# A retention and two-layer MLP kernel on one core: each load of q, k, n, v and raw weights waits for an older load

## Chip, core and metric

The kernel runs on one core of one Trainium2 chip. The metric is the device time of one execution in microseconds (us), as a median over executions. TensorE (PE) multiplies matrices, VectorE (DVE), ScalarE (ACT) and GpSimd (POOL) work on tiles in SBUF, and SyncE (SP) computes nothing here: it issues transfers (DMAs), one after the other, in program order. An instruction on SP that waits for a semaphore holds up every transfer that is queued behind it on SP.

## The reference, cut to what matters

```
for t in range(S):                       # B, H, S, D = 2, 8, 768, 64
    state = gamma * state + einsum('bhd,bhe->bhde', k[:, :, t], v[:, :, t])
    y[:, :, t] = scale * einsum('bhd,bhde->bhe', q[:, :, t], state)
x = y.transpose(0, 2, 1, 3).reshape(1536, 512)
x = ((x @ w_a) * (x @ w_b)) @ w_out                  # 512 -> 1536 -> 512
h = x @ w_in                                          # 512 -> 2048
out = maximum(0.01 * h, h) @ moe2_w_out               # 2048 -> 512
```

All inputs and the output are float32.

## The kernel before

The work has three stages. The first one, retention, is done in 12 units: three tiles of 512 tokens by four pairs of heads. Each unit needs four tiles of 128x512 float32 (256 KB each): q and k (transposed), n (k in its plain layout) and v. The second stage is the product with w_a and w_b, the product of the two results and the product with w_out; the third is the last two products. Products are written as three matmuls over a high and a low part of each operand, and from the second stage on many are regrouped so that seven block products do the work of eight.

The weights arrive as raw 64-bit-typed tiles of 128x512 elements (512 KB each), named raw_a, raw_b, raw_wo, raw_wi and raw_wq. ACT and DVE turn each raw tile into a float32 tile; there are NRAW = 4 raw buffers, and `load_weights` issues the next raw load when one comes free.

`manual_schedule` is on, so each engine runs its instructions in the order in which the Python program emits them. All the loads of this case are issued on SP. `loads(u)` (line 519) issues the four loads of unit u, in the order q, k, n, v for units 0 to 3 and n, v, q, k for the others. The program starts with the loads of units 0 to 4, then the raw loads a0, b0 and a1 among the loads of units 5 and 6, and in the main loop (line 1067) unit u calls `loads(u + 8)`, the first pass also `load_weights()`. In all, 48 loads of 256 KB and six of 512 KB (a0, b0, a1, b1, a2, b2) are issued before 46 us. The framework gives the transfers of SP and ACT eight semaphores in turn, and a transfer waits for the one that had the same semaphore before it. Two transfers of ACT (table and rest, small constants) share these semaphores at the start.

The first matmuls of the second stage (line 1016, pa and pb) run inside the retention stage, as soon as the weights a0 and b0 are split and unit 3 is done. Here ACT's lines 316, 318 and 320 and DVE's lines 334, 336 and 338 turn a raw tile into float32; ACT's line 989 and DVE's line 996 split it; ACT's lines 539 and 603 scale n; POOL's and DVE's lines 545 and 608 scale q.

After the loads of unit 11 and the raw tiles a2 and b2, SP's queue holds only raw loads, tiles that were parked in DRAM and are fetched back (farh, farg, wi, wq; lines 454 and 777), and the stores of the output.

Of the kernel before, what the change touches and what calls it, by code (L numbers as in the profile page):

```python
# [35 lines left out]
NRAW = 4  # L36
NEXTRA = 10
NWARM = 10
FILL = {4: 4, 5: 6, 6: 6, 7: 6, 8: 6, 9: 6, 10: 6, 11: 4}
PUMP = {7: 1.2, 8: 1.6, 9: 1.2, 10: 1.2, 11: 1.2}  # L40
ROUND = {3: ("a", 0, 3), 4: ("b", 0, 3), 5: ("a", 1, 3), 6: ("b", 1, 3)}
# [50 lines left out]
class Seven:  # L92
# [41 lines left out]
    def sum(self, queue, op, j, d, x0, x1, here=False):  # L134

        run = self.nc.vector.tensor_add if op == "+" else self.nc.vector.tensor_sub
        if d[0] == "B":
            queue.append((0.34, lambda: run(*(self.B(*x[1:], j) for x in (d, x0, x1)))))
            return
        for piece, cost in enumerate((0.61, 0.34)):  # L140
            if self.away(*d[1:], j) and not piece:
                continue
            if here:
                queue.append((cost, lambda piece=piece: run(*(self.A(*x[1:], j)[piece] for x in (d, x0, x1)))))
                continue
            queue.append((0.0, lambda piece=piece: self.nc.gpsimd.dma_start(  # L146
                self.A(*d[1:], j)[piece], self.A(*x1[1:], j)[piece], accum_op=ALU.add
            )))
# [81 lines left out]
def retention_moe_kernel(ctx: ExitStack, tc: tile.TileContext, ins, out):  # L230
    nc = tc.nc
# [44 lines left out]
    first_layer = len(order)  # L276
    order += second
    source = {"a": (wab, 0), "b": (wab, 1), "wo": (wo, 0), "wi": (w2, 0), "wq": (w2, 1)}
    raws, begun, rounded, dram = {}, {}, {}, {}
    at = {"load": 0, "begin": 0, "round": 0, "queued": 0, "hold": True}  # L280

    def wait_for(later, done):
        tc.add_manual_dep(
            later.ins, done.ins.name,
            mybir.DependencyInfo(mybir.DependencyClass.Sync, mybir.DependencyReason.DATA),
        )

    def load_weights(behind=()):
        if at["load"] < len(order) and at["load"] < at["round"] + NRAW:
            kind, f = order[at["load"]]  # L290
            src, i = source[kind]
            t = rawp.tile([P, TT], I64, tag="raw", name=f"raw_{kind}{f}")
            load = nc.sync.dma_start(t, src[f, i])
            if behind:
                wait_for(load, behind[-1])
            raws[kind, f] = t
            at["load"] += 1
# [26 lines left out]
    def round_steps():  # L324


        n = at["round"]
        key = order[n]
        if key not in begun:
            begin_weights()  # L330
        u, sl = begun.pop(key)
        raws.pop(key)
        ui = u.bitcast(I32)
        nc.vector.tensor_scalar(u, u, TOP, None, op0=ALU.min)
        yield
        nc.vector.tensor_scalar(ui, ui, 3, None, op0=ALU.logical_shift_left)
        yield
        nc.vector.tensor_tensor(ui, ui, sl, op=ALU.add)
        rounded[key] = u
        at["round"] += 1  # L340
        if not at["hold"]:
            load_weights()
        if key in parked:
            dram[key] = park.tile([P, TT], F32, tag=f"{key[0]}{key[1]}", name=f"{key[0]}{key[1]}")
            nc.gpsimd.dma_start(dram[key], rounded.pop(key))
            slots.done(1)
# [160 lines left out]
    units = [(n, p) for n in range(NTILE) for p in range(NPAIR)]  # L507
# [11 lines left out]
    def loads(u):  # L519
        if u >= len(units):  # L520
            return
        d = un[u] = {}
        source = {"q": qT, "k": kT, "n": kn, "v": vn}
        for name in "qknv" if u < NPAIR else "nvqk":
            d[name] = slots.new(F32, f"{name}{u}")
            nc.sync.dma_start(d[name], source[name][units[u]])

    flip = heads[::-1]
    cols = [slice(j * P, (j + 1) * P) for j in range(CPT)]
# [434 lines left out]
    nc.vector.memset(warm, 0.0)  # L964
    nc.scalar.dma_start(table, head)
    loads(0)
    nc.scalar.copy(carry[0][0][:, 0:1], warm[:, 1:2])
    nc.scalar.dma_start(rest, more)
# [3 lines left out]
    def keep_warm(n):  # L972
        for _ in range(n):
            nc.tensor.matmul(wps, warm[:, 0:P], warm, start=True, stop=True)

    keep_warm(NWARM)
    for u in range(1, 4):
        loads(u)
    loads(4)
    load_weights()  # L980
    loads(5)
    load_weights()
    loads(6)
    load_weights()
# [78 lines left out]
    def fill(u):  # L1063
        for _ in range(FILL.get(u, 0)):
            next(dense)
# [258 lines left out]
    for n in range(NMADE, len(z.plan) - 2):  # L1324
# [12 lines left out]
        name, j = z.plan[n]  # L1337
# [195 lines left out]
    for n in range(NMADE2, len(z.plan) - 2):  # L1533
# [14 lines left out]
        name, j = z.plan[n]  # L1548
# [80 lines left out]
```

## Time and profile before

| | |
|---|---|
| median of 3 runs | 557.0 us (556.24 to 559.15) |
| profiled execution, its own time | 557.07 us |
| span of the profile | 555.3 us |
| granted TensorE clock | 1.0 |
| PE busy | 548.9 us (99%) |
| DVE, ACT, POOL busy | 457.5, 385.8, 158.9 us |
| moved by all DMAs | 108.19 MB, of them 66.60 MB from SP's queue |

The span runs from the first instruction to the last one of the profiled execution; 1.8 us of that execution's time lie outside it. Times in the rows are counted from the start of the span.

### The profile page before, as it was taken

The numbers are of one execution on the slowest core, as the hardware profiler recorded it, in microseconds if no ns is written. First come the engines' busy times: TensorE is split into PE (matmuls) and PEld (weight loads), VectorE is DVE, ScalarE is ACT, GpSimd is POOL, SyncE is SP. The second block draws the span as 40 slices with busy tenths as digits, with TensorE's granted clock in tenths as the row PEclk, the third lists the DMA queues.
The fourth block names the chain that finished last, engine by engine and source line by source line (L and its number), as shares of the span: only waits on it lengthen the run. The fifth ranks groups of instructions, "written<-read, shape, count | busy, mean of one in ns | idle before, by whom it ended". The sixth has DMA issues, their size and how long they took to land.

```text
span 555.3 us, 10484 instructions
## 1 busy us (share of the span) xinstructions
PE 548.9 (99%) x3743; PEld 462.5 (83%) x3743; DVE 457.5 (82%) x973; ACT 385.8 (69%) x797; POOL 158.9 (29%) x203
## 2 busy tenths in 40 slices
PE   8999999999999999999999999999999999999997
PEld 5878888888888888888888888888888888888886
DVE  4877967889898898899789859896977798999862
ACT  4867377877789888867758457769766886687800
POOL 3524201113231430267520320221433556700000
PEclk9999999999999999999999999999999999999999
DMA  8996934548788987899992362665787799964111
GB/s 313 393 375 167 217 93 119 154 133 212 195 253 219 259 220 253 260 305 240 243 186 94 66 125 71 184 181 158 231 240 233 206 272 242 223 164 118 58 58 57
DMA packets 49765, 108.19 MB, mean 195 GB/s; under 512 B 5936, under 2 KB 13360, under 8 KB 49712
## 3 DMA queue, kind: packets, MB, share of 16 engines
q1 hardware_dynamic: 27360, 66.60, 36.7%
q0 software_dynamic: 22064, 40.64, 34.5%
q8 instruction: 29, 0.48, 0.3%
q10 hardware_dynamic: 288, 0.28, 0.2%
q14 instruction: 24, 0.20, 0.1%
HBM read 73.68 MB, written 18.35 MB: 166 GB/s over the span
## 4 chain that ended last, share of the span: by engine, by line
PE 95%; DMA 3%; DVE 1%; issue 0%; ACT 0%; SPq 0%
PE blk L258 12%; PE blk L257 12%; PE blk L259 12%; PE top L257 6%; PE top L258 5%; PE top L259 5%; PE pa L257 4%; PE pa L259 4%; PE pa L258 4%; PE pb L257 4%; PE pb L259 4%; PE pb L258 4%; PE mid L257 3%; PE mid L259 3%; PE mid L258 3%; DMA q<-in_qT 2%
## 5 line engine op out<-in xcount | busy, mean ns | idle before, releaser
L258 PE MATMUL blk<-form,form 128*128 128x512 f32 (+1 forms) x224 | 75.8, 339 | 0.0
L257 PE MATMUL blk<-form,form 128*128 128x512 f32 (+1 forms) x224 | 75.6, 337 | 0.0
L259 PE MATMUL blk<-form,form 128*128 128x512 f32 (+1 forms) x224 | 75.3, 336 | 0.0
L173 DVE TENSOR_TENSOR form<-g,form 128x512 fp32r<-128x512 f32 x112 | 57.6, 551 | 0.9
L258 PE MATMUL blk<-forma,forma 128*128 128x512 f32 (+1 forms) x168 | 56.9, 338 | 0.0
L257 PE MATMUL blk<-forma,forma 128*128 128x512 f32 (+1 forms) x168 | 56.7, 337 | 0.0
L259 PE MATMUL blk<-forma,forma 128*128 128x512 f32 (+1 forms) x168 | 56.4, 336 | 0.0
L167 ACT CAST form<-g 128x512 fp32r<-128x512 f32 x112 | 52.4, 512 | 4.7 <-DMA g<-g 2.8
L257 PEld LDWEIGHTS blk<-form,form 128*128 128x128 f32 x224 | 42.5, 190 | 5.3
L173 DVE TENSOR_TENSOR forma<-h,forma 128x512 fp32r<-128x512 f32 x84 | 43.0, 551 | 4.5 <-ACT forma L167 3.0
L258 PEld LDWEIGHTS blk<-form,form 128*128 128x128 f32 x224 | 42.5, 190 | 4.7
L259 PEld LDWEIGHTS blk<-form,form 128*128 128x128 f32 x224 | 42.3, 189 | 4.8
L167 ACT CAST forma<-h 128x512 fp32r<-128x512 f32 x84 | 38.8, 511 | 2.8 <-DMA h<-h 2.8
L763 POOL DMA_DIRECT2D farg<-g x26 | 15.6, 616 | 80.7 <-ACT g L1373 62.8
L146 POOL DMA_DIRECT2D h<-h x33 | 33.0, 1133 | 14.3 <-DVE forma L173 3.9
L257 PEld LDWEIGHTS blk<-forma,forma 128*128 128x128 f32 x168 | 31.9, 190 | 3.9
L258 PEld LDWEIGHTS blk<-forma,forma 128*128 128x128 f32 x168 | 31.9, 190 | 3.6
L259 PEld LDWEIGHTS blk<-forma,forma 128*128 128x128 f32 x168 | 31.7, 189 | 3.6
L763 POOL DMA_DIRECT2D farh<-h x19 | 11.0, 576 | 74.6 <-DVE h L893 50.3
L173 DVE TENSOR_TENSOR form<-wq,form 128x256 fp32r<-128x256 f32 x56 | 23.4, 418 | 10.0 <-ACT form L167 9.9
L167 ACT CAST form<-wq 128x256 fp32r<-128x256 f32 x56 | 22.6, 403 | 6.3 <-PE blk L258 2.8
L146 POOL DMA_DIRECT2D g<-farg x22 | 22.0, 1040 | 9.1 <-DVE form L173 5.6
(3062 smaller groups left out, 1680.4 us busy)
## 6 DMA issues: line engine op xcount, KB each, us to landing
raw_wi<-in_w SPq DMA_DIRECT2D x16, 512.0 KB, 4.3
raw_wq<-in_w SPq DMA_DIRECT2D x16, 512.0 KB, 5.0
farg<-g POOLq DMA_DIRECT2D x26, 256.0 KB, 4.5
g<-farg SPq DMA_DIRECT2D x26, 256.0 KB, 6.6
raw_a<-in_wab SPq DMA_DIRECT2D x12, 512.0 KB, 4.5
raw_b<-in_wab SPq DMA_DIRECT2D x12, 512.0 KB, 4.9
raw_wo<-in_wo SPq DMA_DIRECT2D x12, 512.0 KB, 5.0
g<-farg POOLq DMA_DIRECT2D x20, 256.0 KB, 8.8
```

The source lines that it names most:

```text
L146: queue.append((0.0, lambda piece=piece: self.nc.gpsimd.dma_start(self.A(*d[1:], j)[piece], self.A(*x1[1:], j)[piece], accum_op=ALU.add)))
L167: nc.scalar.copy(h, src)
L173: nc.vector.tensor_sub(*todo.pop(0))
L257: nc.tensor.matmul(ps, w[0], x[0], start=first, stop=False, skip_group_check=more)
L258: nc.tensor.matmul(ps, w[0], x[1], start=False, stop=False, skip_group_check=more)
L259: nc.tensor.matmul(ps, w[1], x[0], start=False, stop=last, skip_group_check=more)
L763: nc.gpsimd.dma_start(self.far[t, f], self.tiles[t, f])
```

## The change

Each load of q, k, n, v and each raw load is entered in a list with its size in units of 256 KB (1, or 2 for a raw tile). When the loads behind the oldest one of the list, the new load among them, come to FLYING = 5 units or more, the new load waits until the oldest has landed, and the list is shortened until the rest is under 5 units. In a row of 256 KB loads, each so waits for the fifth before it. A raw load among them waits for the fifth before it too; since it counts as two, the next three loads wait for the fourth before them, and the one after these has no such wait of its own. In a row of raw loads alone, each waits for the third before it. Other transfers are neither counted nor made to wait by the list.

```diff
+FLYING = 5
...
-    raws, begun, rounded, dram = {}, {}, {}, {}
+    raws, begun, rounded, dram, aloft = {}, {}, {}, {}, []
...
+    def fly(load, size):
+        aloft.append((load, size))
+        if sum(n for _, n in aloft[1:]) >= FLYING:
+            wait_for(load, aloft.pop(0)[0])
+            while sum(n for _, n in aloft[1:]) >= FLYING:
+                aloft.pop(0)
...
             load = nc.sync.dma_start(t, src[f, i])
+            fly(load, 2)
             if behind:
                 wait_for(load, behind[-1])
...
-            nc.sync.dma_start(d[name], source[name][units[u]])
+            fly(nc.sync.dma_start(d[name], source[name][units[u]]), 1)
```

## Rows read from the trace of the kernel before

**Rows 1.** The page, part 1: busy us, share, instructions.

```profile
PE 548.9 (99%) x3743; PEld 462.5 (83%) x3743; DVE 457.5 (82%) x973; ACT 385.8 (69%) x797; POOL 158.9 (29%) x203
```

**Rows 2.** By stretches: us; PE, PEld, DVE, ACT, POOL busy; PEclk, DMA share, GB/s.

```profile
10.00:15.00 5.00, 4.58 (x88) 3.96 (x86) 2.94 (x7) 3.45 (x9) 2.55 (x2) 1.00 1.06 398
...
5.00:45.00 40.00, 37.97 (x836) 31.52 (x835) 31.08 (x73) 28.16 (x56) 15.45 (x15) 1.00 1.02 377
...
46.00:555.30 509.30, 506.09 (x2896) 428.79 (x2894) 424.49 (x897) 356.17 (x739) 141.03 (x180) 1.00 0.70 181
```

**Rows 3.** The chain that ended last, its start: start us, us, what.

```profile
2.59 5.28 DMA q<-in_qT
7.88 5.51 DMA q<-in_qT
13.41 6.65 DMA raw_a<-in_wab
20.09 0.69 ACT a L316
```

**Rows 4.** SP's timeline, issues of loads: start us, us, what.

```profile
12.05 0.33 SPq L526 DMA_DIRECT2D q<-in_qT  x1
12.73 0.33 SPq L526 DMA_DIRECT2D k<-in_kT  x1
13.41 0.33 SPq L293 DMA_DIRECT2D raw_a<-in_wab  x1
...
25.61 0.33 SPq L293 DMA_DIRECT2D raw_b<-in_wab  x1
...
37.09 0.33 SPq L526 DMA_DIRECT2D v<-in_vn  x1
...
40.28 0.38 SPq L293 DMA_DIRECT2D raw_b<-in_wab  x1
...
208.85 0.33 SPq L293 DMA_DIRECT2D raw_wo<-in_wo  x1
...
215.86 0.33 SPq L293 DMA_DIRECT2D raw_wq<-in_w  x1
```

**Rows 5.** DMA issues of 0-1, 1.6-2, 8-13 us: KB, median us to landing.

```profile
q<-in_qT SPq DMA_DIRECT2D x1, 256.0 KB, 3.2
...
n<-in_kn SPq DMA_DIRECT2D x1, 256.0 KB, 4.2
...
q<-in_qT SPq DMA_DIRECT2D x2, 256.0 KB, 5.8
```

**Rows 6.** The same of 497 to 500 us and of 119 to 119.5 us.

```profile
g<-farg SPq DMA_DIRECT2D x4, 256.0 KB, 2.7
...
raw_a<-in_wab SPq DMA_DIRECT2D x1, 512.0 KB, 3.1
```

**Rows 7.** The same at 25.6, 34 to 38.5, 40.3 and 208.9 us.

```profile
raw_b<-in_wab SPq DMA_DIRECT2D x1, 512.0 KB, 6.6
...
v<-in_vn SPq DMA_DIRECT2D x1, 256.0 KB, 5.1
...
raw_b<-in_wab SPq DMA_DIRECT2D x1, 512.0 KB, 6.0
...
raw_wo<-in_wo SPq DMA_DIRECT2D x1, 512.0 KB, 5.9
```

**Rows 8.** ACT's timeline, first use of raw a0, b1 and b2.

```profile
20.09 0.68 ACT L316 ACTIVATE a<-raw_a 128x512 f32<-128x512 f32 x1 [0.43 <-DMA raw_a<-in_wab]
...
33.84 0.70 ACT L316 ACTIVATE b<-raw_b 128x512 f32<-128x512 f32 x1
...
48.92 0.68 ACT L316 ACTIVATE b<-raw_b 128x512 f32<-128x512 f32 x1
```

## The prediction

> **What bounds the kernel now.** I read the page's busy times first: PE is busy for 548.9 of 555.3 us [rows 1]. Then I asked for busy time by stretches, to find where the missing 6.4 us are. From 46 us on PE idles for 509.30 - 506.09 = 3.2 us, which are spread over 500 us [rows 2]; between 5 and 45 us it idles for 40.00 - 37.97 = 2.03 us; the rest lies ahead of the first data. So two different kernels stand one behind the other: 46 us of retention, in which the DMA engines are as full as PE (a share of 1.06 and 398 GB/s between 10 and 15 us, 377 GB/s as a mean from 5 to 45 us), and 509 us in which PE alone sets the pace, with 181 GB/s beside it [rows 2]. The granted clock is 1.00 in all these stretches.
>
> The third view is the chain that ended last. Up to 20 us it is nothing but loads: a q issued at 2.59 that takes 5.28 us, a q issued at 7.88 that takes 5.51, and raw_a issued at 13.41 that takes 6.65; then ACT turns raw_a into float32 [rows 3]. This chain has to be read with care. Each of its links is the eighth transfer behind the one before: the issue at 7.88 comes 0.01 us after the landing of the load of 2.59, because it takes over that load's semaphore. So the queue is limited already, to eight loads or 2 MB, and SP is not ahead of the engines by more. The 5 to 7 us from issue to landing are then mostly time in the queue: loads are issued 0.68 us apart in the steady stretch (12.05, 12.73, 13.41 [rows 4]), eight of them make 5.4 us, and the view of DMA issues gives 5.8 us to landing there [rows 5]. What sets the time of a landing is how many bytes go before it, and not how early it was asked for.
>
> **The change part by part.** It removes no transfer, changes no size and no order; it adds waits on SP. There are two places to look at: the 54 loads before 46 us, and the raw loads after.
>
> After 46 us a raw load waits for the third before it. The tightest place that I found is the raw_wq issued at 215.86: the third before it is the raw_wo issued at 208.85 [rows 4] that takes 5.9 us [rows 7], so it lands at 214.75, 1.1 us before its successor would be issued anyway. All the others have more, since a raw load waits for a raw buffer and so for ACT's work. Sum of this part: 0. The cover is that buffer wait; were it gone, at most these raw loads would go out some us later, 10 us and more ahead of their use in a queue that runs behind PE.
>
> Before 46 us the waits do bite: eight loads in flight become five. (Around a raw tile, which counts as two, it is up to six units, 1.5 MB; the bound is not sharp.) The waiting instruction holds up all that is queued behind it on SP, and until 46 us these are only the next loads. Now the question is whether the engines run dry. Five loads 0.68 us apart cover 5 x 0.68 = 3.4 us. A load starves the engines only if it needs more than that from its issue to its landing when nothing is ahead of it in the queue. No row shows five in flight at full rate, so I bound it. From below: 2.7 us, for loads of the same 256 KB from a nearly empty queue [rows 6]. From above: 4.2 us, for the third load of the program [rows 5]; it has two loads and the two tables ahead of it, so a good part of that is queue. Between the two lies the very first load, with 3.2 us [rows 5], with ACT's two table loads beside it. I take the value that the row of the empty queue gives, since that row measures just the part that isn't queue, with SP, the engines and the landing in it: 2.7 us, 0.7 under the 3.4. The queue then never runs dry, loads land 0.68 us apart as before, and each at its old time. Only the time to landing falls, from 5.8 to about 3.4 us. The first five loads are issued as before, so the start is the same too.
>
> I check the late side for the last loads. The raw tile b2 now waits for v of unit 11, which is issued at 37.09 [rows 4] and takes 5.1 us [rows 7]: it goes out at 42.2 in place of 40.28. With the 3.1 us of a raw tile in an empty queue [rows 6] it can land at 45.3; before, it landed at 40.28 + 6.0 = 46.3 [rows 4, 7], and ACT takes it up at 48.92 [rows 8]. Hidden, with over 2 us to spare.
>
> What does a landing cost if it does come late? The raw tile a0 has no cover: ACT waits 0.43 us for it [rows 8], and its chain leads on to PE. The 17 units of 256 KB from the q that lands at 7.87 (2.59 + 5.28) to raw a0, landing at 20.06 (13.41 + 6.65 [rows 3]), make 12.2 us, so each 0.01 us more per load costs 0.17 us. Later tiles have some cover: raw b1 lands at 25.61 + 6.6 = 32.2 [rows 4, 7] and is taken up at 33.84 [rows 8], 1.6 us later.
>
> Sum: 0 + 0 + 0, on a profiled execution of 557.07 us (555.3 of span and 1.8 around it), which is the median of the runs, 557.0.
>
> **A rule that speaks against it.** The rows say that 2.7 us of a load are not queue [rows 6], but they say it at a low load. The Trainium skill, DMA: Bandwidth & Descriptors, section "Latency and other measured facts", gives the HBM access latency as 0.2 us on average and 2 us at high load. An estimate by that page would put the time of a lone load at 2.7 + 1.8 = 4.5 us at full rate, over the 3.4, so 0.90 us per load; raw a0 would be 17 x 0.22 = 3.7 us late and raw b1 35 x 0.22 - 1.6 = 6.1 us, and the kernel would take some 563 us. No row here shows five loads in flight at full rate, so the trace can't refute it; this is the first rival.
>
> **The rivals.**
> *The engines starve* (slower). The mechanism: time to landing at full rate is over 3.4 us even with a short queue; from there on, each load costs a fifth of it. Against it speaks the 2.7 us; for it, that the first load took 3.2 us, and that nothing shows a loaded engine. At the upper bound of 4.2 us it is 0.84 per load, 0.16 more. Raw a0 then is 17 x 0.16 = 2.7 us late: 559.7. If the delay lasts up to raw b1, 35 units after that q, it is 35 x 0.16 - 1.6 of cover = 4.0 us: 561.0. With 3.5 us, just over the edge, it is 0.02 x 17 = 0.3 us, which nobody sees. Chance 0.11.
> *The shorter queue makes landings more even* (faster). From 7.87 to 20.06 the 17 units took 12.2 us, where 17 x 0.68 are 11.6: some 0.6 us went to irregular landings. If fewer loads in flight cure that, raw a0 lands earlier, but ACT gains only its wait of 0.43 us: 556.6. The ceiling is all the idle time of PE between 5 and 45 us, 2.03 us: 555.0. Nothing in the rows says that the depth causes the irregularity. Chance 0.09.
> *The change does not do what it says.* Its waits might be met already by the eight semaphores. The eight are looser than the five, so the waits bite; but the time would be 557.0 as well. Chance 0.03.
>
> **How the numbers follow.** My forecast, the queue stays full and nothing moves, has a chance of 0.77, and gives 557.0. The range reaches down to all of PE's idle time in the first stage recovered, 555.0, and up to raw a0 late by the upper bound, 559.7, to which I add a little for the runs of before that themselves lie between 556.24 and 559.15: 555.0 to 560.0. What is left out above is starvation that lasts to raw b1. About 0.5%, 2.8 us, is what a measurement of this kernel can tell from no change. Faster by more would need more than all the 2.03 us, so 0.04 for what I have not seen. Slower by more needs starvation near the upper bound or beyond: 0.08 of the 0.11. Within 0.5%: 0.88.
>
> **What would show it.** Right: between 8 and 13 us the time to landing falls from 5.8 to 3.3 to 3.6 us, SP still issues loads about 0.68 us apart, the stretch 10 to 15 us still moves over 385 GB/s, raw a0 is issued near 15.5 or 16 and not at 13.41 but ACT takes it up between 19.6 and 20.6, and the span from 46 us on is unchanged. Starvation would show as a DMA share well under 1 between 10 and 30 us with loads 0.75 us or more apart, and raw a0 taken up after 21. The prediction is wrong if raw a0 comes at its old time and the end has moved all the same: then the waits cost something on another engine, or past 46 us, that I have not seen.

## The result, and the profile of the kernel after

The kernel after takes 561.83 us in the median of 7 runs (559.18 to 563.5), the kernel before 557.0 us (556.24 to 559.15; the 3 runs known ahead of the prediction and 4 more). The ratio is 1.0082, with a 95% interval of 1.0065 to 1.0100: slower by 4.8 us. Its profiled execution took 562.0 us, with a span of 560.2 us.

Busy time by stretches of the kernel after, with the columns of [rows 2]; the second line is the stretch from 20 to 25 us, which was not shown before:

```profile
10.00:15.00 5.00, 4.58 (x77) 3.96 (x78) 2.90 (x8) 3.58 (x9) 2.01 (x2) 1.00 0.87 292
20.00:25.00 5.00, 4.13 (x88) 3.33 (x84) 2.31 (x7) 2.85 (x7) 2.39 (x3) 1.00 0.85 262
5.00:45.00 40.00, 37.85 (x773) 30.52 (x775) 29.05 (x68) 25.66 (x52) 13.93 (x14) 1.00 0.93 308
46.00:560.20 514.20, 509.32 (x2910) 430.08 (x2902) 427.56 (x904) 358.61 (x743) 142.99 (x181) 1.00 0.69 184
```

The DMA engines are no longer full: 292 GB/s between 10 and 15 us where there were 398, 262 between 20 and 25 us where there were 392, and 308 as a mean from 5 to 45 us where there were 377 [rows 2]. PE's share of busy time from 5 to 45 us hardly differs (37.85 us, before 37.97), but it got through 773 matmuls in that time and not 836: a busy PE there is not a PE at its pace. So the idle time of PE, on which I had set the bounds, does not show the loss; the count of instructions in the stretch does.

The chain that ended last, in its first 50 us (start us, us, what), where [rows 3] stood before:

```profile
3.86 4.51 DMA k<-in_kT
...
8.44 4.42 DMA n<-in_kn
12.87 4.08 DMA v<-in_vn
...
16.96 5.63 DMA raw_a<-in_wab
...
22.61 4.55 DMA raw_b<-in_wab
...
27.18 5.16 DMA raw_a<-in_wab
...
32.35 5.92 DMA raw_b<-in_wab
```

Each link is now the fifth load behind the one before it; the change does what it says. But the links are 4.1 to 4.5 us long for 256 KB, and not 3.4. From the k that lands at 8.37 to raw a0 at 22.59 there are 16 units of 256 KB in 14.2 us, 0.89 us each; to raw b1 at 38.27 there are 34 in 29.9 us, 0.88 each. Five of them make 4.4 us.

ACT's timeline of the kernel after (start us, us, what, idle time before and its releaser), which answers to [rows 8]:

```profile
22.62 0.67 ACT L325 ACTIVATE a<-raw_a 128x512 f32<-128x512 f32 x1 [2.10 <-DMA raw_a<-in_wab]
...
38.34 0.71 ACT L325 ACTIVATE b<-raw_b 128x512 f32<-128x512 f32 x1 [1.41 <-DMA raw_b<-in_wab]
...
53.04 0.67 ACT L325 ACTIVATE a<-raw_a 128x512 f32<-128x512 f32 x1 [1.97 <-DMA raw_a<-in_wab]
...
56.70 0.69 ACT L612 ACTIVATE kd<-n,rest 128x512 f32<-128x512 f32 x1
...
78.61 0.62 ACT L815 CAST s41h<-xf 128x512 fp32r<-128x512 f32 x1 [2.50 <-DMA xf<-xf]
```

Raw a0 is taken up 2.5 us later than before, raw b1 4.5 us later. The last three lines are places where I had not looked at all. Raw a2 had 2.3 us of room before: it landed at 44.8, and ACT took it up at 47.08 without a wait for it:

```profile
47.08 0.68 ACT L316 ACTIVATE a<-raw_a 128x512 f32<-128x512 f32 x1
```

Now ACT waits for it, and behind it stands the scaling of n of unit 10 (kd), for which PE then waits. And at 78.61 ACT waits for the last of eight transfers (xf) that GpSimd issues.

GpSimd's timeline, its queue between 50 and 72 us, and the DMA issues at 70.0 us (KB, us to landing):

```profile
50.87 1.28 POOL L617 TENSOR_TENSOR qs<-q,grown 128x512 f32<-128x512 f32 x1 [1.75 <-DMA q<-in_qT]
52.09 2.17 POOL L1194 DMA_DIRECT2D xf<-xf  x2
...
70.05 0.86 POOL L1194 DMA_DIRECT2D xf<-xf  x1 [3.44 <-DMA xf<-xf]
```

```profile
raw_a<-in_wab SPq DMA_DIRECT2D x1, 512.0 KB, 3.9
xf<-xf POOLq DMA_DIRECT2D x1, 256.0 KB, 8.5
```

GpSimd scales q of unit 11 first (its load landed at 50.7, before at 42.9), and then adds tiles of x onto one another with eight transfers, some of which wait for others of them. Before, the first was issued at 46.43 and the last landed at 67.7; now they are 52.09 and 78.5. The last one alone took 4.0 us before, from its issue at 63.71 to its landing:

```profile
xf<-xf POOLq DMA_DIRECT2D x1, 256.0 KB, 4.0
```

There the raw loads a4 and b4 ran beside it too, but were issued 1.2 and 1.7 us behind it (64.94 and 65.37); in the kernel after they go out 0.1 us ahead of it and 0.3 us behind it (69.93 and 70.35, against 70.05).

To see where PE falls behind I took the start of the same matmul in each trace (PE runs the same 3743 in the same order). Start in the kernel before in us, then how much later it is in the others, each in its one profile (kv are a unit's products of n and v, x is its output, a block is a product of the second stage):

```
                        before  after  head  late_a2  late_xf  a0_late
unit 4, first x          23.11   +2.5  +2.9    +0.7     +0.3     +2.6
ahead of unit 9          48.20   +1.8  +2.5    -0.0     -0.5     +1.7
unit 10, first kv        54.94   +2.5  +2.4    +2.3     -0.4     +1.6
unit 11, 1st block       72.70   +3.0  +2.4    +2.8     -0.4     +1.6
second fast block        95.59   +4.9  +2.4    +3.0     +0.9     +1.6
in the rest             213.62   +5.0  +2.5    +2.9     +1.0     +1.7

                         after  after2  apart  apart2   f6     f4
unit 4, first x           +2.5   +2.3   +2.6   +4.8   +0.1   +3.8
ahead of unit 9           +1.8   +2.5   +2.1   +4.3   -0.3   +4.1
unit 10, first kv         +2.5   +5.1   +4.2   +6.2   -0.2   +8.8
unit 11, 1st block        +3.0   +5.7   +5.7   +6.8   +0.4  +10.1
second fast block         +4.9   +5.9   +5.7   +7.0   +1.8  +10.1
in the rest               +5.0   +6.0   +5.7   +7.1   +1.9  +10.0
```

The other columns belong to the experiments. Single runs scatter (the seven of the kernel after lie between 559.18 and 563.5; the profile of before is itself a run of 557.07, and later medians of that kernel lay between 556.55 and 557.21), so the jumps within a column say more than its level. In the kernel after there are two large jumps: 2.5 us at the first tiles, part of it made up, and 1.8 us between the first block of unit 11 and the second fast block (the second of those that do with seven products what took eight, and need the tiles that the xf transfers make). Behind that nothing changes until the end.

### The profile page after: what moved, and what is told of

Read it like the earlier page. It is cut to its first block, busy times and chain, and to the rows that moved or that the text cites. A ratio compares the mean times of both kernels' runs of the same rounds, so it can differ in the third digit from the quotient of the medians.

```text
span 560.2 us, 10485 instructions
## 1 busy us (share of the span) xinstructions
PE 552.0 (99%) x3743; PEld 462.9 (83%) x3743; DVE 458.6 (82%) x973; ACT 385.7 (69%) x797; POOL 159.1 (28%) x203
## 4 chain that ended last, share of the span: by engine, by line
PE 82%; DMA 13%; ACT 2%; DVE 1%; issue 1%; POOL 0%; ACTq 0%; POOLq 0%; SPq 0%
PE blk L259 12%; PE blk L258 12%; PE blk L260 12%; PE top L258 5%; PE top L259 5%; PE top L260 5%; DMA xf<-xf 4%; PE mid L258 3%; PE mid L260 3%; PE mid L259 3%; PE pb L260 3%; PE pa L260 3%; PE pb L259 3%; PE pa L259 3%; PE pa L258 3%; PE pb L258 3%
```

## The experiments

Each ratio is taken to runs of the kernel before on the same chip.

### The disputed cost by itself: loads at depths from one to eight

A kernel that only loads the 48 tiles of q, k, n and v over and over (260 loads), with so many in flight, and stores one of them twelve times; none of the computation is done. It ran once.

```diff
...
+            load = nc.sync.dma_start(t, s[n, p])
+            if i >= depth:
+                wait_for(load, here[i - depth])
+            elif made:
+                wait_for(load, made[-1])
```

> This kernel does none of the computation: it only loads the q, k, n and v tiles of 256 KB from SP, 40 at a time with eight, seven, six, five and four in flight (30 with three, 20 with two, 10 with one), each load waiting for the one so many before it, and stores one tile as the output. Theory 1 (a load needs about 4.4 us from issue to landing as soon as the engines are at full rate, so five in flight cover 0.87 us per load): loads 0.67 to 0.70 us apart with eight and seven, 0.73 with six, 0.87 with five, 1.1 with four, 2.7 with one. Theory 2 (a load needs 2.7 us at any rate, and the loss in the kernel comes from what runs beside the loads there): 0.67 to 0.70 us apart with eight, seven, six, five and four, 0.9 with three, 1.35 with two, 2.7 with one.

Stretches of this kernel with 1, 2, 3, 4, 5, 6, 7 and 8 loads in flight (us, POOL busy, PEclk, DMA share, GB/s):

```profile
2.00:26.00 24.00, 0.00 (x0) 1.00 0.35 100
282.00:302.00 20.00, 0.00 (x0) 1.00 0.65 184
250.00:272.00 22.00, 0.00 (x0) 1.00 0.83 254
215.00:238.00 23.00, 0.00 (x0) 1.00 0.89 286
173.00:194.00 21.00, 0.00 (x0) 1.00 0.95 317
133.00:152.00 19.00, 0.00 (x0) 1.00 0.96 351
93.00:111.00 18.00, 0.00 (x0) 1.00 1.05 391
50.00:70.00 20.00, 0.00 (x0) 1.00 1.03 380
```

It takes seven loads in flight, not five, to fill the engines: five bring 317 GB/s of 391. Where the time goes can be read from the semaphores in the same trace. Each load raises its semaphore sixteen times, and there are sixteen DMA engines; I read each rise as one engine that is done. Median times after the issue, over the loads behind the first ones of each depth:

```
in flight                 1     2     3     4     5     6     7     8
first of 16, us          2.24  2.26  2.37  2.45  2.59  3.11  4.08  4.10
last of 16 (landed), us  2.65  2.78  2.99  3.70  3.98  4.30  4.72  5.40
us between landings      2.64  1.42  1.02  0.92  0.82  0.72  0.67  0.67
```

Up to five in flight, the first engine is done 2.2 to 2.6 us after the issue, hardly later than for a load alone; there is no queue to speak of. But a load has landed when its last engine is done, and the sixteen drift apart: the last one is 0.4 us behind the first with one load in flight, and 1.4 with five. A window that opens when the last engine is done leaves the engines that were done earlier without work. That is only about half of the loss. With five in flight the engines are still busy for a share of 0.95, where seven give 1.05, but they move 317 GB/s and not 391, so single packets must take longer too. In the trace's records of the packets (2 KB each, same stretches) one takes 97 ns in the mean with five in flight and 87 with seven, while the median is 84 and 86: a few are slow, the longest 1.05 us with five and 0.31 with seven.

Theory 2 falls: nothing runs beside the loads here, and five don't suffice. Theory 1 holds for five and more (0.82 and 0.72 for 0.87 and 0.73 expected), but a load does not need 4.4 us as soon as the engines are busy: with four it is 3.7, with three 3.0. That makes 0.92 us per load with four, not 1.1. In the kernel five cost 0.17 us more per load than before (0.89 for 12.2 / 17 = 0.72), here 0.15 more than seven, so the loads alone account for nearly all of it; why both figures of the kernel lie 0.05 to 0.07 higher was not tried. Why some packets are slow, and whether it is always the same engine that is done last, stays open as well.

### The depth in the kernel

Only the number is changed:

```diff
-FLYING = 5
+FLYING = 8
```

and likewise to 7, 6 and 4.

> FLYING = 8 in place of 5: in a row of 256 KB loads each waits for the eighth before it, as the semaphores make it do already. If the waits cost time only through the depth of the queue: 557.0, within 0.7 us of the kernel before, and raw a0 taken up at 20.1 us. If the added waits cost something by themselves on SP or elsewhere: 559 or more.

> FLYING = 7. From the loads measured alone (0.68 us per load with seven in flight, as with eight, 0.72 with six, 0.82 with five): the queue stays full, 556 to 557 us, no difference to the kernel before. If the loads in the kernel need more than 7 x 0.68 = 4.8 us: 557.5 or more.

> FLYING = 6. Theory 1 (4.4 us per load, shared by six): 0.73 us per unit, raw a0 taken up near 21.0 us, 558 us in all. Theory 2 (2.7 us per load, the loss comes from single late landings, which six in flight cover hardly better than five): most of the loss stays, raw a0 after 22 us, 560.5 or more.

> FLYING = 4. Theory 1: 4.4 us shared by four are 1.1 us per unit, 17 x 0.38 = 6.5 us later than before at raw a0, taken up near 26.5 us, and some 12 us more in all, 569 us. Theory 2 (2.7 us per load, four cover 0.68 us each): the queue just holds, and only single late landings add to the loss: 562 to 565 us.

Measured: 8 gives 556.06 us, ratio 0.9989 (0.9979 to 0.9998); 7 gives 556.42, 0.9996 (0.9983 to 1.0009); 6 gives 558.92, 1.0038 (1.0023 to 1.0053); 4 gives 567.75, 1.0203 (1.0186 to 1.0220). With eight the same waits are there, and cost nothing; with seven it is they that hold the loads (41 of the loads ahead of 52 us go out within 0.1 us of the landing that the list names, 2 at that of their semaphore), and they cost nothing either. So the loss of five is one of depth. The edge lies between seven and six, where the loads measured alone have it too. With four it is 11 us, near the 12 of theory 1 and far over theory 2, but theory 1 has the number by luck: ACT takes raw a0 up at 23.94 us, not near 26.5, and PE's first x of unit 4 is 3.8 us late, not 6.5. Of the 11 us, 4.7 come at unit 10 (+4.1 to +8.8 in the table), in one wait for ACT's kd. The 6 came out otherwise than either theory had it: raw a0 is in time (PE's first x of unit 4 is 0.1 us late in the table), and yet the kernel is slower by 2.1 us; the table has most of it between the first block of unit 11 and the second fast block. So a second way in which late loads cost time is to be looked for at the end of the loads.

### The first loads alone, and the last loads alone

The limit holds only for the first 36 loads, up to raw b1 (head), or only for those behind them (tail):

```diff
     def fly(load, size):
+        flown.append(load)
+        if not 0 < len(flown) <= 36:      # tail: not 36 < len(flown) <= 1000
+            return
```

> The kernel after, with the limit only on the first 36 loads (units 0 to 7 and the raw tiles a0, b0, a1, b1); the loads behind them are limited by the eight semaphores alone. If the loss is made by the first tiles being late, raw a0 above all, and is carried to the end: 561 to 562 us, as with the whole change. If it is made by the late end of the loads (raw a2 and unit 11, and the xf transfers that follow on GpSimd): the queue catches up after the 36th load, and 558 to 559 us.

> The kernel after, with the limit only on the loads behind the 36th (units 8 to 11 and the raw tiles from a2 on). If the loss is made by the first tiles: 557.0 us, no difference. If it is made by the late end of the loads: about 20 units that take 0.2 us more each, so the last ones land some 4 us late, and 558.5 to 560 us.

Measured: head 559.47 us, ratio 1.0048 (1.0032 to 1.0063), some 2.7 us; tail 557.08 us, 0.9999 (0.9987 to 1.0011). The first tiles alone carry 2.7 of the 4.8 us. The last loads alone cost nothing, but the two parts together cost 2 us more than their sum: the late end of the loads has room, and the late start seems to use it up first. Neither of my two expectations for head had this middle value; the closer one is the second, and for a reason that it did not have.

### Raw a0 late, and nothing else

The kernel before, with raw a0 loaded behind unit 5 and not ahead of it:

```diff
     loads(4)
-    load_weights()
     loads(5)
     load_weights()
+    load_weights()
```

> The kernel before, without any limit, with raw a0 loaded behind the four loads of unit 5 in place of ahead of them; raw a0 lands some 2.6 us later, as in the kernel after, and the loads of unit 5 some 1.4 us earlier. Theory 1 (a late raw a0 moves PE one for one, and that stays): 559.0 to 559.6 us. Theory 2 (a late raw a0 alone is partly made up by PE's idle time up to 37 us, since b0, a1, b1 and the later units come at their old times): 557.8 to 558.6 us. No cost (the wait is hidden after all): 556.7 us.

Measured: 559.37 us, ratio 1.0040 (1.0026 to 1.0055), 2.4 us. ACT takes raw a0 up at 22.69 in that profile, as late as in the kernel after. By the median this is theory 1. The table shows 2.6 us at the first matmuls and 1.6 us from the next units on in the profiled run (558.69 us), which is theory 2; this one run lies below the median, and the two can't be told apart by it. That a late raw a0 by itself costs about what the whole limit on the first 36 loads does (2.7 us) holds either way.

### The end of the loads: the xf transfers late, and nothing else

The kernel before; the first xf transfer waits for ACT's high part of x of unit 8:

```diff
...
-                nc.gpsimd.dma_start(xf[d], xf[a], accum_op=ALU.add)
+                moved = nc.gpsimd.dma_start(xf[d], xf[a], accum_op=ALU.add)
+                if highs:
+                    wait_for(moved, highs[8])
+                    highs.clear()
```

> The kernel before, without any limit; only the first of the eight accumulating xf transfers on GpSimd waits for ACT's high part of x of unit 8, which ends near 52 us, so that the transfers start about 5.7 us later, as they do in the kernel after. If the second half of the loss, some 2 us, comes from these transfers ending late: 558.5 to 559.5 us, and the last xf lands after 73 us. If they have that much room: 557.0 us.

Measured: 558.35 us, ratio 1.0028 (1.0015 to 1.0041), 1.6 us, just under the range that I gave. The transfers started 6.9 us later, at 53.34, and not 5.7. The last xf lands at 74.5 us, 2.2 us after PE starts the first block of unit 11 (72.3); in the kernel after it is 2.8 us (78.5 and 75.7), and in the kernel before it landed 5.0 us ahead of that. The table has the whole loss between this block and the second fast one, +1.3 us. ACT works in order, so it waits ahead of the splitting of that tile and can't do the work behind it. Its timeline:

```profile
74.63 0.62 ACT L808 CAST s41h<-xf 128x512 fp32r<-128x512 f32 x1 [1.54 <-DMA xf<-xf]
```

### Raw a2 and b2 late, and nothing else

The kernel before; the two raw loads wait for ACT's copy of x of unit 7:

```diff
...
             copy_x(u)
+            if u == 7:
+                load_weights(copied)
+                load_weights(copied)
...
-        if u in (5, 6, 8, 9, 10, 11):
+        if u in (8, 9, 10, 11):
```

> The kernel before, without any limit, in which the raw loads a2 and b2 wait for ACT's copy of x of unit 7, which ends near 46.7 us; a2 then lands near 50 us in place of 44.8, which against PE's work is about as late as in the kernel after. Theory (ACT runs its instructions in order, so the scaling of n of unit 10 and with it PE's states of that unit stand behind the rounding of a2 and b2): PE waits about 2 us near 55 us, and the kernel takes 558 to 559 us. Rival (a2 and b2 have that much room): 556.7 us.

Measured: 559.88 us, ratio 1.0046 (1.0033 to 1.0059), 2.6 us, over the 558 to 559 that I gave. Raw a2 landed at 51.8 us, not near 50. In the kernel after it landed at 53.0, with PE 1.8 us late ahead of unit 9, and in that kernel's second profile (after2, below) at 54.7, with PE 2.5 us late; against PE's work 51.8 lies between the two. PE's waits in this run (waiter, releaser, us in total, times, longest us):

```profile
PE kv L675 <- ACT kd L603: 2.3, 1, 2.3
```

So the end of the loads has two ways to cost time, 1.6 and 2.6 us by themselves, and each is about as large as the 2 us that head leaves open.

### Taking one of the two away, and repeats

The kernel after, with the raw loads a4 and b4 behind the last xf transfer, so that this one has no raw loads beside it:

```diff
...
             fly(load, 2)
+            if (kind, f) in (("a", 4), ("b", 4)):
+                wait_for(load, moved[7])
```

> The kernel after (FLYING = 5), in which the raw loads a4 and b4 also wait for the landing of the last xf transfer, so that they no longer run beside it. Theory: the second part of the loss, 1.8 us, is the last xf landing (after: 78.5 us) behind the point at which PE needs what is made of it (75.8 us), and it lands so late because it shares the engines with a4 and b4 (8.5 us, before 4.0). Then it lands near 74 us, and the kernel takes 560.0 us. Rival (the late start of the xf transfers alone is enough, or the raw loads, now later, cost as much themselves): 561.8 us or more.

Measured: 562.05 us, ratio 1.0093 (1.0080 to 1.0106); my 560.0 was wrong. The profile shows the link that I had named gone, and no gain from it: the last xf takes 3.5 us, lands at 76.7 us, 1.7 us before PE starts the first block of unit 11, and the jump behind that is 0. But PE had lost more before, at unit 10. The edit can't have done that, since a4 and b4 are issued long behind it, at 70 us in the kernel after. Both kernels were therefore run again side by side.

> The kernel after once more, unchanged, beside the next one on the same chip. If the two late ends (PE waiting near 57 us for the scaling behind raw a2, and PE waiting between 76 and 101 us for what the xf transfers make) take each other's place from run to run, with the sum fixed: 561.8 us again, with more of one and less of the other in this profile.

> The variant with a4 and b4 behind the last xf once more, unchanged. If its first result (562.0 us, no gain) was a matter of the chip or the hour: near 560.0 us. If taking a4 and b4 away from the xf transfers does not help since the wait behind raw a2 is the longer of the two: 562 us again, and the wait near 57 us over 1.5 us.

Measured: after2 562.65 us, 1.0096 (1.0080 to 1.0111); apart2 561.82 us, 1.0083 (1.0052 to 1.0114). PE's waits in after, after2, apart and apart2, one line from each:

```profile
PE kv L684 <- ACT kd L612: 0.7, 1, 0.7
```

```profile
PE kv L684 <- ACT kd L612: 2.6, 1, 2.6
```

```profile
PE kv L687 <- ACT kd L615: 2.1, 1, 2.1
```

```profile
PE kv L687 <- ACT kd L615: 1.9, 1, 1.9
```

and what stands ahead of that kd on ACT in after2:

```profile
54.68 0.66 ACT L325 ACTIVATE a<-raw_a 128x512 f32<-128x512 f32 x1 [3.54 <-DMA raw_a<-in_wab]
...
57.51 0.66 ACT L325 ACTIVATE b<-raw_b 128x512 f32<-128x512 f32 x1 [0.85 <-DMA raw_b<-in_wab]
...
59.31 0.71 ACT L612 ACTIVATE kd<-n,rest 128x512 f32<-128x512 f32 x1
```

The same program lost 0.7 us at unit 10 and 1.8 us at the xf transfers in its first profile, and 2.6 and 0.2 us in its second. So the larger wait at unit 10 in apart is scatter between runs, and the smaller jump at the xf transfers needs no edit: in after2 the last xf landed at 77.2 us, 1.2 us ahead of the first block of unit 11. A reading that fits the four profiles is that the two are not a sum: when raw a2 and b2 land late, PE comes later to the fast blocks, and the xf transfers have landed by then, so that the kernel pays some 2 to 3 us for both. It is argued from one profile each and was not tried by itself. What is shown is that the variant gains nothing, in two medians of four runs.

## Why the prediction was wrong

The first view, the two stages of the kernel, was read rightly, and so was the chain: it has one link for each window of loads, and the limit shortens the window from eight to five. The cost past 46 us was rightly put at nothing: behind b2, one raw load alone goes out right at the landing of the third before it (220.91 and 220.85 us). It is the raw_wq for which I had found 1.1 us of room; that raw_wo now took 7.0 us, not 5.9. PE's delay is 5.0 us there, and the two spans differ by 4.9.

The step that failed is the time to landing with five in flight. I took 2.7 us, "since that row measures just the part that isn't queue", from loads in an almost empty queue [rows 6], 0.7 us under the 3.4 that five loads cover. Alone on the engines it is 2.65 us with one in flight, and 3.98 us with five. In the kernel after it is 4.4 us for five units. My upper bound of 4.2 us, from the third load of the program [rows 5], was near the truth, and I explained it away as queue. The row that I chose had the right size of transfer, but came from a time when the engines were almost idle; "no row shows five in flight at full rate" should have moved the value toward the upper bound, and the chance of that rival well over 0.11.

The rival itself was worked out nearly right: 0.84 us per load (0.88 measured), raw a0 2.7 us late (2.5), ACT's start on raw b1 4.0 us late (4.5), 559.7 to 561.0 us (561.83). That its 561.0 lies so near is luck, since what it adds to the 2.7 us for raw a0 is not what made up the rest. The first of its terms is shown: the limit on the first 36 loads costs 2.7 us, and a late raw a0 alone 2.4. The second, that the delay grows on to raw b1, is not: in head raw b1 lands at 38.6, as late as in the kernel after, and the loss stays at 2.7.

The Trainium skill, DMA: Bandwidth & Descriptors, section "Latency and other measured facts", has the HBM access latency at 2 us at high load; my estimate by it was 4.5 us for a load. The runs agree in size, with 4.0 us alone and 4.4 us in the kernel for five in flight, and differ in form: the time to landing does not come with full rate, but grows with each load in flight (2.65, 2.78, 2.99, 3.70, 3.98 us). No run here tells how much of it is HBM access.

"Hidden, with over 2 us to spare" failed too. I checked raw b2 against the time at which it is taken up, with loads ahead of it that come at their old times; the loads of 36 to 46 us came 8 us late, and the cover was gone. And I named what is queued behind the waiting loads on SP, but not what stands behind their users on in-order engines: ACT's kd behind the rounding of raw a2, and GpSimd's eight transfers behind the scaling of q of unit 11. By head, late_xf and late_a2 these are the other 2 us, and no case of mine had them.

The bound from PE's idle time was no bound. PE's busy time from 5 to 45 us was the same within 0.12 us, with 63 matmuls fewer, so time that is lost can stand inside busy time.

Of the signs that I gave, these decide: time to landing between 8 and 13 us is 4.2 to 4.5 us in the kernel after (not 3.3 to 3.6), the DMA share 0.85 between 20 and 25 us, loads 0.88 us apart, and raw a0 taken up at 22.62.

## What to carry to other kernels

How many loads a queue needs in flight is to be measured at full rate, by the landing of the slowest DMA engine; the time of a lone load is a lower bound that here was short by a third. A limit that costs little per load is paid where the loads end: look for what waits on the last of them, and for what stands behind that on each in-order engine. When two waits can hide one another, mending one may show nothing; each must be tried alone in the kernel without the fault. FLYING at 7 is no better than the kernel before (0.9996), and at 8 it is 0.1% better (0.9989, with an interval that ends at 0.9998), so there is hardly anything here to gain from the limit.

## What the runs showed of the hardware that was not expected

With loads of 256 KB from one queue, 3 in flight move 254 GB/s, 5 move 317 and 7 move 391; by the rises of the semaphores, the engine that is done first keeps its 2.2 to 2.6 us up to five, while the last of the sixteen goes from 2.65 to 3.98 us. A transfer of 256 KB that adds onto its target took 3.5 us with no raw load beside it (apart), 4.0 us where two raw loads of 512 KB were issued 1.2 and 1.7 us behind it (before), and 8.5 us where they went out 0.1 us ahead of it and 0.3 us behind it (after).
